# Windowed attention with sinks and a max-of-three FFN on one core: the opening in another order, its masks on TensorE, Q turned in one transfer

## The chip, the core and the metric

The kernel runs on one core of a Trainium2 chip. The core has a matmul engine (TensorE, PE), a vector engine (VectorE, DVE), a scalar engine that also evaluates exp (ScalarE, ACT), a general engine (GpSimd, POOL) and a sync engine that here only issues transfers (SyncE, SP). Each takes its instructions in order; what they hand over goes through semaphores. Sixteen DMA engines move data between HBM and on-chip memory. ScalarE, GpSimd and SyncE can issue transfers; those that change the type on the way (weights, float32 to bfloat16) are issued from GpSimd here. The metric is device time in microseconds, the median over runs. Lower is better.

## The reference

Attention over 4 batches, 8 heads, 768 positions, 64 dimensions. A position sees the first 4 positions (sinks) and the last 128. The result, as 3072 tokens of 512 features, goes through three projections to 768 features, their elementwise maximum, and a projection back:

```python
scores = scale * np.matmul(q, k.transpose(0, 1, 3, 2))
keep = is_sink | in_window            # pos < 4, or 0 <= rel < 128
a = softmax(np.where(keep, scores, -1e9))
x = (a @ v).transpose(0, 2, 1, 3).reshape(B * S, H * D)
h = np.maximum(np.maximum(x @ w1, x @ w2), x @ w3)
out = h @ w_out
```

## The kernel before

The work is cut into 12 chunks of 256 positions, three per batch (chunk `ci` is part `c = ci % 3` of batch `b`). A chunk has two blocks of 128 queries; heads go in four pairs `p`. All engines' orders are the order in which the program emits the calls; nothing is rescheduled, but each engine runs ahead of the others as far as its semaphores let it.

The steps of a chunk, each a function:
- `load` (L67) fetches k, q, v in float32, 512 KB each, into `k_raw`, `q_raw`, `v_raw` (two buffers each, so chunk `ci` waits for the casts of `ci - 2`).
- `cast_qk`, `cast_v` (L86, L95) make bfloat16 copies, in two and four instructions, from chunk 2 on GpSimd.
- `turn` (L100) transposes k and q on TensorE, with a copy out by VectorE (k) or ScalarE (q); `turn_dma` (L113) does it with DMA transposes issued by SyncE, two for k and two for q, 64 partitions each. `kT`, `qT` and `vb` are rings of four.
- `score` (L199) writes transposed scores (keys on partitions) of a pair into two banks `st`; `expo` (L218) takes the exponential on ScalarE and multiplies it by a 0/1 mask (`msk`, for a batch's first chunk `msk0`) on VectorE.
- `sink_k` (L176, GpSimd) copies the first four keys of a batch into `ks`; `sink_score` (L225) gives scores against them for the chunks that are not a batch's first, `sink_v` (L239) gathers the values of these keys.
- `av_open`, `av` (L251, L266) multiply with v, with the sum of the weights as a 65th column; VectorE takes the reciprocal and scales into `x_sb`.
- `xpose` (TensorE, copies by ScalarE) or `xpose_dma` (one DMA transpose) turn x into `xT`.
- `ffn_h(ci, fp, wi)` (L307) is one third of one projection: 8 matmuls of 256 columns; ScalarE copies the first projection to `h_sb`, VectorE takes the maximum with the others. `ffn_y` (L326) is half of the output projection, 6 matmuls of 512 columns, copied out by ScalarE; `store` (L335) issues the output.

PSUM has 8 banks, given out in turn; a bank's ninth user waits for the first to be read.

The opening (L350 to L433) is written out by hand for chunks 0 to 2. Masks are made by GpSimd first. Chunk 0's k halves are fetched from SyncE's queue and its q halves from ScalarE's. Casts of chunk 0 stand on VectorE. The four weights are issued by GpSimd, two behind chunk 0's v casts, one behind chunk 1's q casts, and the last (`wo`) behind chunk 1's v casts. Chunk 2's loads have a gate: VectorE writes one element of each buffer first, behind the mask products of chunk 1's second pair. Chunks 3 and 4 follow as buffers come free.

From L435 a loop does iteration `i` from 2 to 11: casts of chunk `i+2`, loads of `i+3`, DMA turns of `i+2`, then, with `n = i + 1`, `sink_k` and `sink_v` where `n` is the second chunk of a batch, sinks and scores of `n`, the output projection of `i - 1`, exponentials of `n`, projections of `i` mixed with `av` of `n`, and x of `n` turned by DMA. On GpSimd `sink_k` therefore stands behind the casts of chunk `i + 2`, and on TensorE `sink_score(n)` and all behind it wait for `ks`.

Of the kernel before, what the change touches and what calls it, by code (L numbers as in the profile page):

```python
# [16 lines left out]
def kernel(  # L17
# [31 lines left out]
    with tc.manual_schedule():  # L49
# [10 lines left out]
        qT = [const.tile([128, 2, NP, 2, 64], BF16, name=f"qT{i}") for i in range(RING)]  # L60
# [6 lines left out]
        def load(ci, what="kqv", eng=None, parts=1, gate=None):  # L67
# [4 lines left out]
            for w in what:  # L72
                src = {"k": k, "q": q, "v": v}[w]
                if (ci, w) not in raws:
                    raws[ci, w] = raw.tile([128, H, 2, D], F32, tag=w + "_raw", name=w + "_raw")
                dst = raws[ci, w]
                if gate is not None:
                    gate.memset(dst[0:1, 0, 0, 0:1], 0.0)
                n = H // parts
                for g in range(parts):  # L80
                    (eng or nc.sync).dma_start(
                        out=dst[:, n * g:n * g + n],
                        in_=src[b, n * g:n * g + n, t0:t0 + 256]
                            .rearrange("h (p i) d -> p h (i d)", i=2))
# [15 lines left out]
        def turn(ci, w, g):  # L100

            pt = bank([128, 2, 2, 128], BF16, "pt")
            x = bfs[ci, w]
            for p in range(2):
                for i in range(2):
                    nc.tensor.transpose(  # L106
                        pt[:, p, i], x[:, 2 * g + p, i].rearrange("q a d -> q (a d)"), ident)
            dst = (kT if w == "k" else qT)[ci % RING]
            (nc.vector.tensor_copy if w == "k" else nc.scalar.copy)(
                dst[:, :, 2 * g:2 * g + 2].rearrange("q n p i r -> q n (p i) r"),  # L110
                pt.rearrange("q p i (n r) -> q n (p i) r", r=64))

        def turn_dma(ci, w):  # L113
            dst = (kT if w == "k" else qT)[ci % RING]
            x = bfs[ci, w].rearrange("q p i a d -> q (p i a d)")
            for n in range(2):
                nc.sync.dma_start_transpose(  # L117
                    out=dst[:, n].rearrange("q p i r -> q (p i) r"), in_=x[64 * n:64 * n + 64])
# [8 lines left out]
        sel = const.tile([128, 32], BF16, name="sel")  # L127


        msk = const.tile([128, 2, 4, 128], BF16, name="msk")  # L130
        msk0 = const.tile([128, 2, 3, 128], BF16, name="msk0")

        def masks():
            nc.gpsimd.memset(msk[:, 0, 0:2], 1.0)
            for i in range(2):
                hp = slice(64 * i, 64 * i + 64)
                nc.gpsimd.affine_select(
                    out=msk[hp, 0, 1], in_=msk[hp, 0, 1], compare_op=ALU.is_ge, fill=0.0,
                    base=-i, pattern=[[1, 2], [2, 64]], channel_multiplier=-2)
                nc.gpsimd.affine_select(  # L140
                    out=msk[hp, 0, 0], in_=msk[hp, 0, 0], compare_op=ALU.is_gt, fill=0.0,
                    base=i, pattern=[[-1, 2], [-2, 64]], channel_multiplier=2)
            nc.gpsimd.tensor_copy(msk0[:, 0, 0], msk[:, 0, 1])
            nc.gpsimd.tensor_copy(msk0[:, 0, 1], msk[:, 0, 0])
            nc.gpsimd.tensor_copy(msk0[:, 0, 2], msk[:, 0, 1])
            for i in range(2):
                nc.gpsimd.memset(msk0[64 * i:64 * i + 2, 0, 0:2], 1.0)
            nc.gpsimd.tensor_copy(msk0[:, 1], msk0[:, 0])

        def masks_late():  # L150
            nc.gpsimd.tensor_copy(msk[:, 0, 2:4], msk[:, 0, 0:2])
            nc.gpsimd.tensor_copy(msk[:, 1], msk[:, 0])

        bm = const.tile([128, 2], F32, name="bm")

        def sink_init():

            nc.gpsimd.memset(sel, 0.0)
# [25 lines left out]
        w_sb = []  # L184

        def load_w(wi):
            w = (moe_w1, moe_w2, moe_w3)[wi]
            wt = const.tile([128, DS, d_ff], BF16, name=f"w{wi}")
            nc.gpsimd.dma_start(out=wt, in_=w.rearrange("(a p) f -> p a f", p=128))
            w_sb.append(wt)  # L190
# [8 lines left out]
        def score(ci, pairs):  # L199
            b, c = divmod(ci, CPB)  # L200
            kc, qc = kT[ci % RING], qT[ci % RING]
            for p in pairs:
                st = [bank([128, 4, 128], F32, "st") for a in range(2)]
                for s, x, n, q0, q1 in ((0, kT[(ci - 1) % RING], 1, 0, 1), (1, kc, 0, 0, 2),
                                        (3, kc, 1, 1, 2)):
                    if s == 0 and c == 0:
                        continue
                    for a in range(2):
                        hp = slice(64 * a, 64 * a + 64)
                        nc.tensor.matmul(  # L210
                            st[a][:, s:s + q1 - q0],
                            lhsT=x[hp, n, p].rearrange("q i r -> q (i r)"),
                            rhs=qc[hp, q0:q1, p].rearrange("q n i r -> q n (i r)"),
                            start=True, stop=True)
# [303 lines left out]
```

## Time and profile before

| | |
|---|---|
| median of 3 runs | 205.19 us (204.28 to 205.7) |
| the profiled execution, its own time | 206.73 us |
| its span, first to last instruction | 205.0 us |
| mean granted TensorE clock | 0.958 |
| busy: TensorE, VectorE, ScalarE, GpSimd | 174.1, 111.5, 88.9, 71.9 us |
| HBM read and written | 25.17 MB, 6.29 MB |

How to read it: the rows of digits cut the span into 40 slices of 5.1 us, a digit is the busy share in tenths. A row of the chain of waits is start, duration, engine and what it did. A row of a timeline is start, duration, engine, line, operation, output<-inputs, form, count and, in brackets, how long the engine had stood idle and what ended that. A row of windows is the stretch, its length, then busy time (and instructions) of TensorE's matmuls, its weight loads, VectorE, ScalarE and GpSimd, the granted clock, the DMA share and GB/s. "SPq" and "POOLq" are issues of transfers on the queues of SyncE and GpSimd. The clock row is 1.00 from the start although the first transposes ran slower than later ones (0.62 us for four at 5.19, 0.89 us for sixteen at 43.36), so the early slices of that row are not a reading.

### The profile page before, as it was taken

How to read it: one execution, taken by the hardware profiler on the slowest of the kernel's cores; microseconds unless marked ns; L12 is line 12 of the kernel's file. 1: busy time of each engine (PE TensorE's matmuls, PEld its weight loads, DVE VectorE, ACT ScalarE, POOL GpSimd, SP SyncE). 2: the span in 40 equal slices, each digit the busy share in tenths (PEclk: the TensorE clock that was granted, in tenths of full speed). 3: DMA queues.
4: the chain of work that ended last, by engine and by line, in shares of the span. 5: the costliest groups of instructions: out<-in, count | busy, mean ns of one | idle time of the engine just before them, and what ended most of it. 6: DMA issues, size and time to landing. Idle time of an engine off the chain costs nothing.

```text
span 205.0 us, 4504 instructions
## 1 busy us (share of the span) xinstructions
PE 174.1 (85%) x1788; PEld 129.8 (63%) x1800; DVE 111.5 (54%) x239; ACT 88.9 (43%) x177; POOL 71.9 (35%) x139
## 2 busy tenths in 40 slices
PE   0345978999739999999967999999999899999990
PEld 0223755896624976858735958858678488685860
DVE  1247263264831683864934845937739368286340
ACT  2412772225423537348163148264272661742321
POOL 7298702779204602611802706408227000000000
PEclk9999995799976999999997999999999999999999
DMA  5999999993569829979999989789899963142404
GB/s 153 290 200 204 184 161 290 294 276 105 132 109 299 167 52 252 176 176 295 96 137 294 181 218 243 165 207 244 146 268 167 173 110 99 35 102 51 106 0 102
DMA packets 72436, 35.68 MB, mean 174 GB/s; under 512 B 30176, under 2 KB 69344, under 8 KB 72416
## 3 DMA queue, kind: packets, MB, share of 16 engines
q1 hardware_dynamic: 68992, 31.73, 74.1%
q0 software_dynamic: 2368, 3.15, 9.9%
q10 hardware_dynamic: 1056, 0.52, 1.0%
q8 instruction: 14, 0.23, 0.5%
q14 instruction: 6, 0.05, 0.1%
HBM read 25.17 MB, written 6.29 MB: 153 GB/s over the span
## 4 chain that ended last, share of the span: by engine, by line
PE 48%; DMA 14%; ACT 11%; DVE 10%; issue 8%; SPq 4%; POOL 2%; DVEq 0%
PE h_ps L314 30%; PE y_ps L331 8%; ACT e_sb L222 7%; DMA xT<-x_sb 5%; DMA qT<-q_bf 4%; PE st L210 4%; DVE h_sb L322 3%; DMA q_raw<-in_q_dram 3%; DVE x_sb L285 3%; SPq L117 3%; PE pt L106 2%; PE o L277 2%; DMA k_raw<-in_k_dram 2%; ACT y_sb L333 2%; DVE e_sb L223 2%
## 5 line engine op out<-in xcount | busy, mean ns | idle before, releaser
L314 PE MATMUL h_ps<-xT,w 128*128 128x256 bf16 x864 | 107.1, 280 | 3.2 <-DMA xT<-x_sb 3.2
L314 PEld LDWEIGHTS <-w 128*128 128x128 bf16 x864 | 83.6, 100 | 17.4 <-DMA xT<-x_sb 5.0
L223 DVE TENSOR_TENSOR e_sb<-e_sb,msk 128x1024 bf16<-128x1024 bf16 (+1 forms) x48 | 34.2, 712 | 58.9 <-ACT e_sb L222 55.9
L322 DVE TENSOR_TENSOR h_sb<-h_sb,h_ps 128x512 bf16<-128x512 bf16 x72 | 49.2, 683 | 18.6 <-PE h_ps L314 16.4
L222 ACT ACTIVATE e_sb<-st 128x512 bf16<-128x512 f32 (+1 forms) x96 | 49.4, 585 | 6.3 <-PE st L210 6.3
L320 ACT CAST h_sb<-h_ps 128x512 bf16<-128x512 f32 x36 | 21.6, 601 | 47.8 <-PE h_ps L314 47.8
L91 POOL CAST k_bf<-k_raw 128x512 bf16<-128x512 f32 x20 | 13.4, 694 | 70.6 <-issue 42.0
L331 PE MATMUL y_ps<-wo,h_sb 128*128 128x512 bf16 x132 | 34.2, 392 | 1.1 <-DVE h_sb L322 0.2
L96 POOL CAST vb<-v_raw 64x512 bf16<-64x512 f32 x48 | 31.2, 650 | 10.6 <-DMA v_raw<-in_v_dram 8.6
L331 PEld LDWEIGHTS <-h_sb 128*128 128x128 bf16 x144 | 13.7, 100 | 17.9 <-issue 3.9
L333 ACT COPY y_sb<-y_ps 128x512 f32<-128x512 f32 x24 | 14.2, 592 | 21.8 <-PE y_ps L331 11.0
L285 DVE TENSOR_TENSOR x_sb<-o,rc 128x256 bf16<-128x256 f32 x48 | 20.4, 425 | 1.7
L277 PE MATMUL o<-vb,e_sb 128*128 128x65 bf16 x352 | 18.7, 197 | 1.7 <-DVE e_sb L223 1.7
L210 PE MATMUL st<-qT,kT 64*128 64x128 bf16 (+1 forms) x256 | 15.0, 256 | 4.7 <-DMA qT<-q_bf 2.3
L277 PEld LDWEIGHTS <-e_sb 128*128 128x128 bf16 x352 | 16.3, 100 | 4.1 <-DVE e_sb L223 2.2
L91 POOL CAST q_bf<-q_raw 128x512 bf16<-128x512 f32 x22 | 14.8, 699 | 3.6 <-DMA q_raw<-in_q_dram 3.4
L210 PEld LDWEIGHTS <-kT 64*128 64x128 bf16 x256 | 10.3, 101 | 8.4 <-issue 7.0
L106 PE MATMUL pt<-ident,k_bf 128*128 128x128 bf16 x24 | 3.3, 280 | 8.1 <-DVE k_bf L91 8.1
L296 PE MATMUL xt<-ident,x_sb 128*128 128x128 bf16 x24 | 4.3, 280 | 4.9 <-DVE x_sb L285 4.8
L282 DVE RECIPROCAL rc<-o 128x4 f32<-128x4 f32 x48 | 8.4, 175 | 0.1
L297 ACT COPY xT<-xt 128x512 bf16<-128x512 bf16 x6 | 3.2, 588 | 11.7 <-PE xt L296 11.7
L236 ACT ACTIVATE e_sink<-sk 128x256 bf16<-128x256 f32 x8 | 3.1, 384 | 11.6 <-PE sk L231 11.6
(46 smaller groups left out, 44.1 us busy)
## 6 DMA issues: line engine op xcount, KB each, us to landing
v_raw<-in_v_dram SPq DMA_DIRECT2D x12, 512.0 KB, 7.1
k_raw<-in_k_dram SPq DMA_DIRECT2D x11, 512.0 KB, 5.8
q_raw<-in_q_dram SPq DMA_DIRECT2D x11, 512.0 KB, 6.6
out_dram<-y_sb SPq DMA_DIRECT2D x22, 256.0 KB, 4.0
w<-in_moe_w_dram POOLq DMA_DIRECT2D x3, 768.0 KB, 7.2
wo<-in_moe_w_out_dram POOLq DMA_DIRECT2D x1, 768.0 KB, 9.1
q_raw<-in_q_dram ACTq DMA_DIRECT2D x2, 256.0 KB, 5.0
k_raw<-in_k_dram SPq DMA_DIRECT2D x2, 256.0 KB, 4.4
```

Of the source, the lines that this page charges most:

```text
L91: eng.tensor_copy(x[:, 2 * g:2 * g + 2].rearrange("q p i a d -> q p a i d"), y[:, 4 * g:4 * g + 4].rearrange("q (p a) i d -> q p a i d", a=2))
L96: eng.tensor_copy(vb[ci % RING][64 * i:64 * i + 64, n, :, 0:D], raws[ci, "v"][64 * n:64 * n + 64, :, i])
L210: nc.tensor.matmul(st[a][:, s:s + q1 - q0], lhsT=x[hp, n, p].rearrange("q i r -> q (i r)"), rhs=qc[hp, q0:q1, p].rearrange("q n i r -> q n ...
L222: nc.scalar.activation(e[:, a, lo:], st[a][:, lo:], AF.Exp, scale=scale)
L223: nc.vector.tensor_mul(e[:, :, lo:], e[:, :, lo:], msk0 if lo else msk)
L277: nc.tensor.matmul(o[:, t, a], lhsT=e[:, a, s], rhs=vb[cv % RING][:, n, 2 * p + a], start=first, stop=True, skip_group_check=True)
L285: nc.vector.tensor_mul(xs[ci][:, :, p], o[:, :, :, 0:D], rc.unsqueeze(3).to_broadcast([128, 2, 2, D]))
L314: nc.tensor.matmul(hp[:, f].rearrange("q (t r) -> q t r", t=2), lhsT=w_sb[wi][:, ds, c0:c0 + 128], rhs=xTs[ci][:, :, ds], start=(ds == 0), ...
L320: nc.scalar.copy(dst, hp)
L322: nc.vector.tensor_max(dst, dst, hp)
L331: nc.tensor.matmul(yp, lhsT=hs[ci][:, fb, t * 128:(t + 1) * 128], rhs=wo[:, fb], start=(fb == 0), stop=(fb == FB - 1))
L333: nc.scalar.copy(ys[ci][:, t], yp)
```

## The change

It has five parts.

1. *Masks of chunks 0 and 1.* GpSimd and VectorE build additive masks `addm`, `addm0` (0 or -2^30). `score(..., add=True)` first writes the mask into the banks with a matmul against the identity and adds the scores to it; `expo(..., mul=False)` then leaves out VectorE's product. The 0/1 masks for later chunks are made from the additive ones on GpSimd (`masks_late`), behind the third weight.
2. *Opening order.* All loads of chunks 0 and 1 go out from SyncE's queue. ScalarE casts q of chunks 0 to 3, VectorE k of 0 and 1, and v of 0 and 1 is shared by VectorE and GpSimd. TensorE gets 8, 3 and 6 matmuls on zeros (`warm`) at three places, ScalarE an exponential of one element at the start. The calls of chunks 0 to 3 are written in another order; chunk 3 is turned on TensorE and the loop starts at `i = 3`.
3. *Transfers of the opening.* The first two weights follow GpSimd's half of chunk 0's v casts. Chunk 2's loads are gated by a copy on GpSimd that reads the second weight. The third weight goes in two halves, `wo` behind the k casts of chunk 2, and chunk 3's loads are gated behind the v casts of chunk 2.
4. *Q in one DMA transpose* of 128 partitions in place of two of 64; `qT` is laid out as pair, parity, block, position, and the score and sink matmuls read it with strides.
5. `sink_v` masks by using one selection matrix per head of the pair: 8 matmuls of 65 columns in place of 4 of 130 and a product; `bm` goes.

```diff
-        qT = [const.tile([128, 2, NP, 2, 64], BF16, name=f"qT{i}") for i in range(RING)]
+        qT = [const.tile([128, NP, 2, 2, 64], BF16, name=f"qT{i}") for i in range(RING)]
...
         def turn_dma(ci, w):
+            if w == "q":
+                nc.sync.dma_start_transpose(
+                    out=qT[ci % RING].rearrange("q p i n r -> q (p i) (n r)"),
+                    in_=bfs[ci, w].rearrange("s p i a d -> s (p i a d)"))
+                return
             for n in range(2):
...
-        load(0, "k", nc.sync, 2)
-        load(0, "q", nc.scalar, 2)
-        load(0, "v", nc.sync)
-        load(1, "kqv", nc.sync)
+        load(0, "kq", parts=2)
+        load(0, "v")
+        load(1)
...
+        def warm(n):
+            if n:
+                pw = bank([128, 512], F32, "warm")
+                for _ in range(n):
+                    nc.tensor.matmul(pw, lhsT=wz[:, 0:128], rhs=wz, start=True, stop=True)
...
+        def masks_late():
+            for a in range(2):
+                nc.gpsimd.tensor_scalar(msk[:, a], addm, 2.0 ** -30, 1.0, op0=ALU.mult, op1=ALU.add)
+            for a in range(2):
+                nc.gpsimd.tensor_scalar(msk0[:, a], addm0, 2.0 ** -30, 1.0, op0=ALU.mult, op1=ALU.add)
...
+        def score(ci, pairs, add=False):
...
+            if add:
+                m = addm if c else addm0
+                for p in pairs:
+                    for a in range(2):
+                        nc.tensor.matmul(sts[p][a][:, lo:], lhsT=ident, rhs=m,
+                                         start=True, stop=False, skip_group_check=True)
...
-            nc.vector.tensor_mul(e[:, :, lo:], e[:, :, lo:], msk0 if lo else msk)
+            if mul:
+                nc.vector.tensor_mul(e[:, :, lo:], e[:, :, lo:], msk0 if lo else msk)
...
+        warm(8)
+        masks()
+        sink_init()
         for g in range(2):
+            cast_qk(0, "k", g, nc.vector)
+            cast_qk(0, "q", g, nc.scalar)
+            turn(0, "k", g)
+            turn(0, "q", g)
+            score(0, range(2 * g, 2 * g + 2), add=True)
+        for p in range(NP):
+            expo(0, p, mul=False)
...
         load_w(0)
+        sink_k(0)
         load_w(1)
+        warm(3)
...
+        load_w(2, 0, d_ff // 2)
+        load_w(2, d_ff // 2, d_ff)
+        sink_v(0)
+        for p in range(NP):
+            expo(1, p, mul=False)
+        warm(6)
...
+        masks_late()
+
+        def after_w1(dst):
+            nc.gpsimd.tensor_copy(dst, w_sb[1][0:1, 0, 0:1])
+
+        load(2, gate=after_w1)
...
+        load_wo()
...
+        load(3, gate=pool_gate)
+        load(4)
...
+        store(0)
+        cast(3, q=nc.scalar)
...
+        store(1)
...
+        cast(4)
+        turn_dma(4, "k")
+        turn_dma(4, "q")
...
+        load(5)
...
-        for i in range(2, NCH):
+        for i in range(3, NCH):
```

SyncE's queue around chunk 5's loads (`k_raw_851` and its neighbours before). Before: chunk 4's loads, the store of chunk 0, the turns of chunk 3, then chunk 5's loads and the turns of chunk 4.

```order
L81 DMA v_raw_704<-in_v_dram 128x8x128
L338 DMA out_0_dram<-y_sb_709 64x2x512 x2
L117 DMA_TRANSPOSE kT3_72<-k_bf_690 128x8x64 x2
L117 DMA_TRANSPOSE qT3_76<-q_bf_693 128x8x64 x2
L81 DMA k_raw_851<-in_k_dram 128x8x128
L81 DMA q_raw_853<-in_q_dram 128x8x128
L81 DMA v_raw_855<-in_v_dram 128x8x128
L117 DMA_TRANSPOSE kT0_69<-k_bf_841 128x8x64 x2
L117 DMA_TRANSPOSE qT0_73<-q_bf_844 128x8x64 x2
L338 DMA out_0_dram<-y_sb_892 64x2x512 x2
```

Now (chunk 5's loads are `k_raw_1032` and its neighbours, the two stores those of chunks 0 and 1):

```order
L79 DMA v_raw_635<-in_v_dram 128x8x128
L364 DMA out_0_dram<-y_sb_776 64x2x512 x2
L364 DMA out_0_dram<-y_sb_875 64x2x512 x2
L122 DMA_TRANSPOSE kT0_69<-k_bf_977 128x8x64 x2
L117 DMA_TRANSPOSE qT0_73<-q_bf_980 128x8x128
L79 DMA k_raw_1032<-in_k_dram 128x8x128
L79 DMA q_raw_1034<-in_q_dram 128x8x128
L79 DMA v_raw_1036<-in_v_dram 128x8x128
L327 DMA_TRANSPOSE xT_1109<-x_sb_1060 128x8x128
```

The store of chunk 1 and the turns of chunk 4 moved ahead of chunk 5's loads, the turns of chunk 3 left the queue, and q's turn is one transfer.

GpSimd between the sinks' keys of the first batch and chunk 2's casts. Before, the first two weights (`w0_198`, `w1_200`) have gone out ahead of this piece, right behind chunk 0's four v casts; `q_bf_226` is chunk 1's q, `vb1_78` its v, `w2_230` the third weight, `k_bf_486` chunk 2's k:

```order
L180 COPY ks0_81<-kT0_69 64x4x4 x2
L151 COPY msk_105<-msk_105 128x256
L152 COPY msk_105<-msk_105 128x512
L91 CAST q_bf_226<-q_raw_95 128x2x2x2x64 x2
L189 DMA w2_230<-in_moe_w3_dram 128x4x768
L96 CAST vb1_78<-v_raw_97 64x8x64 x4
L195 DMA wo_108<-in_moe_w_out_dram 128x6x512
L91 CAST k_bf_486<-k_raw_370 128x2x2x2x64 x2
```

Now (`w1_118` is the second weight, `w2_119` the third in halves, `k_raw_498` to `v_raw_504` are chunk 2's buffers, `k_bf_520` its k, `vb2_79` its v):

```order
L195 COPY ks0_81<-kT0_69 64x4x4 x2
L204 DMA w1_118<-in_moe_w2_dram 128x4x768
L94 CAST vb1_78<-v_raw_97 64x8x64 x2
L204 DMA w2_119<-in_moe_w3_dram 128x4x384 x2
L175 TENSOR_SCALAR msk_114<-addm_112 128x512 x2
L177 TENSOR_SCALAR msk0_115<-addm0_113 128x384 x2
L431 CAST k_raw_498<-w1_118 1x1
L431 CAST q_raw_501<-w1_118 1x1
L431 CAST v_raw_504<-w1_118 1x1
L90 CAST k_bf_520<-k_raw_498 128x2x2x2x64 x2
L210 DMA wo_120<-in_moe_w_out_dram 128x6x512
L94 CAST vb2_79<-v_raw_504 64x8x64 x4
```

The sinks' keys moved between the first and the second weight, chunk 1's q casts and half of its v casts left GpSimd, four mask instructions and the three copies that gate chunk 2's loads came in behind the third weight, and `wo` moved behind chunk 2's k casts.

More of the change, by code (lines that the diff above doesn't have):

```diff
@@ L65, with load @@
         raws, bfs = {}, {}
-        def load(ci, what="kqv", eng=None, parts=1, gate=None):
+        def load(ci, what="kqv", gate=None, parts=1):
             if ci >= NCH:
@@ L100, in turn @@
         def turn(ci, w, g):
-            pt = bank([128, 2, 2, 128], BF16, "pt")
+            pt = bank([128, 4, 128], BF16, "pt")
             x = bfs[ci, w]
[L104 to L111, printed above, removed]
@@ L133, in masks @@
         def masks():
[L134 removed]
+            nc.gpsimd.memset(addm[:, 0:2], 0.0)
             for i in range(2):
@@ L378 @@
             av(0, p)
-        xpose(0, 0)
-        xpose(0, 1)
+            if p == 1:
+                for g in range(2):
+                    cast_qk(1, "k", g, nc.vector)
+        for g in range(2):
+            cast_qk(1, "q", g, nc.scalar)
         for g in range(2):
@@ L410 @@
             turn(2, "q", g)
[L411 to L412 removed]
+        ffn_h(1, 0, 2)
         sink_score(2)
[L414 to L416 removed]
+        score(2, (0, 1))
+        score(2, (2, 3))
         for p in range(NP):
             expo(2, p)
[L419 to L424 removed]
+        ffn_h(1, 1, 2)
+        ffn_h(1, 2, 2)
+        ffn_y(0, 0)
         av_open(2)
         av(2, 0)
[L427 removed]
         av(2, 1)
+        ffn_y(0, 1)
         av(2, 2)
[L430 removed]
         av(2, 3)
+        store(0)
+        cast(3, q=nc.scalar)
         xpose(2, 0)
         xpose(2, 1)
[L435 removed]
+        ffn_y(1, 0)
+        ffn_y(1, 1)
+        store(1)
+        for wi in range(3):
+            ffn_h(2, 0, wi)
+        for g in range(2):
+            turn(3, "k", g)
+            turn(3, "q", g)
+        score(3, (0, 1))
+        score(3, (2, 3))
+        cast(4)
+        turn_dma(4, "k")
+        turn_dma(4, "q")
+        expo(3, 0)
+        expo(3, 1)
+        ffn_h(2, 1, 0)
+        expo(3, 2)
+        ffn_h(2, 1, 1)
+        expo(3, 3)
+        ffn_h(2, 1, 2)
+        load(5)
+        ffn_h(2, 2, 0)
+        av_open(3)
+        av(3, 0)
+        av(3, 1)
+        ffn_h(2, 2, 1)
+        av(3, 2)
+        ffn_h(2, 2, 2)
+        av(3, 3)
+        xpose_dma(3)
+        for i in range(3, NCH):
             n = i + 1
             last = n >= NCH
+            load(i + 3)
             cast(i + 2)
[L439 to L442 removed]
+            turn_dma(i + 2, "k")
+            turn_dma(i + 2, "q")
             if not last:
@@ L447 @@
                 sink_score(n)
-                score(n, range(NP))
+                score(n, (0, 1))
+                score(n, (2, 3))
                 expo(n, 0)
```

195 lines of the change are left out of this document (90 added, 105 removed).

## Prediction, made before the changed kernel was run

> **What bounds the kernel now.** I read the page first, then the chain of waits in order of time, then the timelines of each engine up to the steady loop, then windows around the places where TensorE stood. The page:
>
> ```profile
> span 205.0 us, 4504 instructions
> PE   0345978999739999999967999999999899999990
> PEclk9999995799976999999997999999999999999999
> DMA  5999999993569829979999989789899963142404
> ```
>
> TensorE is full in most slices; the open ones are the first six (to 31 us), slice 11 (about 56 to 61) and the tail. The granted clock dips after each early gap. The chain of waits has the durations that I use as prices, and the moment from which both kernels do the same:
>
> ```profile
> 0.82 3.84 DMA k_raw<-in_k_dram
> 5.19 0.62 PE pt L106 x4
> 43.36 0.89 PE pt L106 x16
> 44.25 2.62 PE h_ps L314 x24
> 46.88 0.22 PE sk L231 x4
> 47.10 1.01 PE st L210 x24
> 75.01 0.17 PE sv L244 x4
> ```
>
> At 75.0 (`sv`) the loop body with `i = 3` begins: sinks and scores of chunk 4. The changed kernel reaches the same point with the same chunks finished, so from there both have 205.0 - 75.0 = 130.0 us of the same body, apart from Q's turn. The question is when it gets there. I call that moment T3; 75.0 before.
>
> **The opening on ScalarE.** The timeline of ScalarE before:
>
> ```profile
> 7.29 0.59 ACT L109 COPY qT<-pt 128x512 bf16<-128x512 bf16 x1 [4.06 <-PE pt L106]
> 15.01 1.64 ACT L222 ACTIVATE e_sb<-st 128x384 bf16<-128x384 f32 x4 [0.56 <-PE st L210]
> 20.48 1.07 ACT L297 COPY xT<-xt 128x512 bf16<-128x512 bf16 x2 [3.84 <-PE xt L296]
> 23.69 0.39 ACT L236 ACTIVATE e_sink<-sk 128x256 bf16<-128x256 f32 x1 [0.49 <-PE sk L231]
> 24.22 2.06 ACT L222 ACTIVATE e_sb<-st 128x512 bf16<-128x512 f32 x4 [0.15 <-PE st L210]
> ```
>
> and the windows for the load rate and for the clock:
>
> ```profile
> 2.40:13.00 10.60, 2.65 (x20) 1.54 (x20) 3.95 (x8) 3.06 (x6) 6.33 (x14) 1.00 1.15 285
> 55.60:58.78 3.18, 1.03 (x8) 0.57 (x8) 2.64 (x8) 0.12 (x1) 0.00 (x0) 0.96 0.70 111
> 58.78:65.66 6.88, 5.05 (x28) 2.34 (x27) 0.56 (x1) 2.70 (x7) 1.27 (x3) 0.52 0.95 230
> ```
>
> Moving chunk 0's q load from ScalarE's queue to SyncE's costs order, not bytes: at 285 GB/s a half (256 KB) takes 0.92 us. The first two halves landed at 4.66 after an issue at 0.82, so 2.0 us are latency; q's first half is now third: 0.82 + 2.0 + 3 x 0.92 = 5.6, say 6.0. From there ScalarE is the chain, since it now casts q: cast 0.59 (no row for it on ScalarE; taken as its copy of the same size, bounds 0.4 to 0.9), four transposes 0.62, qT copy 0.59, and the same for the second half: 9.6. Then a score gap of 0.5 and eight exponentials at 0.41: 13.4. Chunk 1: two q casts 1.2, two qT and two xT copies 2.1, sinks 0.39, eight exponentials at 0.51 = 4.1, handoffs 0.6: 21.8. The mask products are gone from this chain; the mask matmuls (8 of 384 and 8 of 512 columns) run on a TensorE that waits for ScalarE, as do the 17 warm-up matmuls, so I cost both at nothing; without that cover they would be 6.8 us (0.11 us for 256 columns by the 2.62 for 24 above). With x of the last pair, transposes and xT copies (2.4, prices below) the dense projections start at 24.3.
>
> **Weights.** The weights' issues on GpSimd, and the transfers' time to landing:
>
> ```profile
> 8.78 3.31 POOL L96 CAST vb<-v_raw 64x512 bf16<-64x512 f32 x4 [3.93 <-DMA v_raw<-in_v_dram]
> 12.04 1.65 POOL L189 DMA_DIRECT2D w<-in_moe_w_dram  x2
> 70.49 0.44 POOL L180 COPY ks<-kT 64x16 bf16<-64x16 bf16 x2
> 158.64 0.44 POOL L180 COPY ks<-kT 64x16 bf16<-64x16 bf16 x2
> DMA to landing us min/median/max: 6.9/7.2/10.0
> ```
>
> Two v casts instead of four stand ahead of the first weight: 8.78 + 1.65 + 0.83 = 11.3, then `sink_k` 0.44, the second weight out by 12.5 and landed by 12.5 + 10.0 = 22.5 at worst. That opens chunk 2's loads. The projections need the first weight at about 19, the second at 26.9 and the third at 32, so it is hidden. The four mask products that GpSimd now makes behind the third weight's issue have no row; between 0.5 and 1.2 each (half and twice its 64x512 cast of about 0.6 to 0.8) they end before 22.5, since v of chunk 1 is there by 13 at the rate above.
>
> **To the loop.** TensorE's and VectorE's prices: the four projection groups ahead of chunk 2's transposes are 4 x 2.62 = 10.5 (34.8), then transposes 0.89, a third of a group 0.87, sinks and scores 1.23: chunk 2's scores end at 37.8; before it was 47.10 + 1.01 = 48.1.
>
> ```profile
> 53.66 0.69 DVE L223 TENSOR_TENSOR e_sb<-e_sb,msk 128x1024 bf16<-128x1024 bf16 x1 [0.29 <-ACT e_sb L222]
> 55.41 0.68 DVE L322 TENSOR_TENSOR h_sb<-h_sb,h_ps 128x512 bf16<-128x512 bf16 x1
> 57.70 0.18 DVE L282 RECIPROCAL rc<-o 128x4 f32<-128x4 f32 x1
> 57.91 0.42 DVE L285 TENSOR_TENSOR x_sb<-o,rc 128x256 bf16<-128x256 f32 x1
> ```
>
> ScalarE's eight exponentials of chunk 2 end 37.4 + 4.1 = 41.5; VectorE's last mask product 42.2, two maxima that stand behind it 43.5, four pairs of reciprocal and product at 0.55 45.7, transposes 46.3. TensorE idles there again, but for shorter than at 56. Two outputs of chunk 1 (12 matmuls of 512 columns at 0.22, 2.7 with the handoff) 49.0, the copy 49.6. On TensorE follow one group 2.62, transposes and copies 1.8, scores 0.8, two groups 5.2 and the products with v 0.7: it is at T3 at about 60.2.
>
> **What is late next.** `sink_k(1)` stands on GpSimd behind the casts of chunk 5, before and after, and TensorE's first score at T3 reads it. SyncE's queue:
>
> ```profile
> 59.03 0.58 SPq L81 DMA_DIRECT2D k_raw<-in_k_dram  x1
> 161.96 2.54 SPq L117 DMA_TRANSPOSE kT<-k_bf  x2
> 164.59 2.54 SPq L117 DMA_TRANSPOSE qT<-q_bf  x2
> 167.22 1.27 SPq L338 DMA_DIRECT2D out_dram<-y_sb  x2
> 172.53 1.25 SPq L301 DMA_TRANSPOSE xT<-x_sb  x1
> ```
>
> Chunk 5's loads went out at 59.03 and `ks` was ready at 70.49 + 0.44 = 70.9: 11.9 us, hidden before, since TensorE came at 75.0. Now they stand behind the store of chunk 1, which waits for that copy at 49.6: store 1.3, kT 2.54, qT 1.25 (one whole-width turn, priced by xT's row): out at 54.8, `ks` at 66.7. So T3 = 66.7, not 60.2; the change moves the wait here. The DMA side does not come ahead of it: gate at 22.8, chunk 2 cast by 22.8 + 11.9 = 34.7, chunk 4's q five parts of 1.84 later and 2.0 latency, 45.9, cast by about 49; its turn is issued at 53.5.
>
> TensorE's 6.5 us idle also cost clock. Timeline of TensorE before:
>
> ```profile
> 60.61 1.47 PE L210 MATMUL st<-qT,kT 64*128 64x256 bf16 x16 [1.61 <-DMA qT<-q_bf]
> 62.84 3.58 PE L331 MATMUL y_ps<-wo,h_sb 128*128 128x512 bf16 x10 [0.22 <-issue]
> 102.81 0.84 PE L210 MATMUL st<-qT,kT 64*128 64x256 bf16 x16 [0.71 <-DMA qT<-q_bf]
> 103.71 2.75 PE L331 MATMUL y_ps<-wo,h_sb 128*128 128x512 bf16 x11
> 108.77 4.40 PE L314 MATMUL h_ps<-xT,w 128*128 128x256 bf16 x24 [2.31 <-DMA xT<-x_sb]
> 159.32 0.29 PE L231 MATMUL sk<-qT,ks 128*32 128x256 bf16 x4 [0.19 <-DMA qT<-q_bf]
> 164.30 2.79 PE L314 MATMUL h_ps<-xT,w 128*128 128x256 bf16 x24 [0.91 <-DMA xT<-x_sb]
> ```
>
> After the gap at 56 scores and outputs took 5.8 (60.61 to 62.84 + 3.58), at full clock 3.65 (102.81 to 103.71 + 2.75): 2.2 lost. [...]
>
> **Q in one transfer.** Each of the seven later chunks frees 2.54 - 1.25 = 1.3 us of SyncE's queue, behind which qT and xT go out. Waits and slow clock behind them in the rows above: 0.71 + 2.31 + (4.40 - 2.79) + 0.91 = 5.5. Each shortened by 1.3 gives 0.7 + 1.3 + 0.9 = 2.9; but `ks`, ready at 158.64 + 0.44 = 159.08, came 0.2 before its user at 159.32, so that round has no more to give. I take 2.0, bounds 0 and 5.5. The strided rows that the scores now read from qT, and `sink_v`'s eight small matmuls instead of four, I cost at 0 to 0.3.
>
> **Sum.** T3 66.7 - 75.0 = -8.3; clock +2.2; Q's turn -2.0: -8.1. The profiled span of 205.0 becomes 196.9, the profiled execution's 206.73 becomes 198.6. That execution was 1.5 above the median of the runs, 205.19; from the median I forecast 205.19 - 8.1 = 197.1.
>
> **Rivals.**
> *The wait for `ks` isn't there* (chunk 5 arrives in time, or its casts are quicker): T3 is TensorE's 60.2, no clock lost, 205.19 - 14.8 - 2.0 = 188.4. For it: nothing but the margins of my chain; against: the 11.9 us row would have to be 5.4. With half the wait it gives about 192. Chance 0.12.
> *Only the opening's gain is real and half of it goes to transfers*: chunk 3's gate and wo's late issue push chunk 4 back by 8 us or more, q's cast holds ScalarE ahead of chunk 2's xT copies. T3 72 to 76 and no gain from Q: 203.1 to 207.2. The DMA share is near full until 48 us in the page's row, which speaks for it; 4 us of slack in the estimate above against. Chance 0.08.
> *Slower: the second weight lands so late that the gate starves the opening.* From its landing L the chain is gate and chunk 2 (12.2), chunks 3 and 4 up to q (11.2), cast and turn (4.6), chunk 5 to `ks` (11.9): T3 = L + 40. That binds above L = 27 and is slower by over 1% from L = 37; at L = 40 T3 is 80 and the time 210.4. Against it: weights landed in 10.0 at most, and it takes 24. [...] Chance 0.06.
>
> **How the numbers follow.** The forecast, with its own range of 192 to 202.5 (T3 from 63.5 to 70.5, clock and Q by their bounds, not all at once), has 0.74. The range 190.5 to 202.5 adds half of the first rival: 0.80. One per cent of the time (2.05 us) is about what a measurement of this kernel can tell from no change. Faster by more than that (under 203.1): forecast and first rival, 0.86; within: 0.08; slower: 0.06.
>
> **What would show it.** Right: the last exponential of chunk 1 near 22 instead of 29; chunk 2's scores done near 38; chunk 5's loads out near 55; a TensorE gap of 4 to 8 us before the first `sk` of chunk 4, ended by GpSimd's `ks` copy, with the granted clock at half behind it; one qT turn of about 1.25 us per chunk on SyncE. Wrong: `sk` of chunk 4 near 60 with no gap (first rival), chunk 2's k cast after 33 or chunk 3's after 45 (the other two), or steady rounds that grow longer without these causes.

## The result: 198.9 us, 2.9% faster, and the profile after

The changed kernel takes 198.88 us (median; 197.69 to 199.98) beside 204.74 for the kernel before in the same comparison: a ratio of 0.971, 95% interval 0.962 to 0.979. The forecast was 197.1 with a range of 190.5 to 202.5. Ratios, here and below, leave disturbed runs out, so they are not always the quotient of the two medians. The profiled execution took 199.98 us, with a span of 198.2 (205.0 before). It is 1.1 us above its kernel's median and that of before 2.0 above, so about 1 us of what lies between the two profiles belongs to the executions.

The page of the changed kernel, the rows that answer to those shown of before:

```profile
span 198.2 us, 4630 instructions
PE   7698969998999079999989999999898999999990
PEclk9999999999999859999999999999999999999999
DMA  5999998998479999349969999799798952122404
```

The open slices at the start are nearly filled. The hole at slice 11 has gone, but there is a new one in slices 13 and 14, 64 to 71 us, with the clock's dip behind it. The timeline of TensorE around it, and its two landmarks ahead:

```profile
28.56 10.64 PE L340 MATMUL h_ps<-xT,w 128*128 128x256 bf16 x96 [0.94 <-ACT xT L323]
41.12 1.06 PE L233 MATMUL st<-qT,kT 64*128 64x128 bf16 x24
...
63.69 0.25 PE L270 MATMUL sv<-vb,sel 128*32 128x65 bf16 x8
70.78 0.41 PE L255 MATMUL sk<-qT,ks 128*32 128x256 bf16 x4 [6.84 <-POOL ks L195]
71.12 1.89 PE L233 MATMUL st<-qT,kT 64*128 64x128 bf16 x24
72.94 3.54 PE L357 MATMUL y_ps<-wo,h_sb 128*128 128x512 bf16 x12
85.57 0.29 PE L255 MATMUL sk<-qT,ks 128*32 128x256 bf16 x4
85.79 1.30 PE L233 MATMUL st<-qT,kT 64*128 64x128 bf16 x24
87.03 2.76 PE L357 MATMUL y_ps<-wo,h_sb 128*128 128x512 bf16 x12
```

TensorE had everything but the sinks' keys at 63.9 and stood 6.84 us for `ks`. The two queues that made it late, SyncE's and then GpSimd:

```profile
48.22 6.59 SPq L364 DMA_DIRECT2D out_dram<-y_sb  x4
54.92 3.19 SPq L122 DMA_TRANSPOSE kT<-k_bf  x2
58.20 1.26 SPq L117 DMA_TRANSPOSE qT<-q_bf  x1
59.52 0.58 SPq L79 DMA_DIRECT2D k_raw<-in_k_dram  x1
```

```profile
23.13 0.18 POOL L431 CAST k_raw<-w 1x1 f32<-1x1 bf16 x1 [3.25 <-DMA w<-in_moe_w_dram]
64.16 1.17 POOL L90 CAST k_bf<-k_raw 128x512 bf16<-128x512 f32 x2 [11.65 <-DMA k_raw<-in_k_dram]
67.66 2.57 POOL L94 CAST vb<-v_raw 64x512 bf16<-64x512 f32 x4 [0.52 <-DMA v_raw<-in_v_dram]
70.29 0.43 POOL L195 COPY ks<-kT 64x16 bf16<-64x16 bf16 x2
```

Stores of chunks 0 and 1 (6.59 us in one piece, the second waiting for its copy), the turns of chunk 4, only then chunk 5's loads at 59.52; their casts hold GpSimd until 70.2, and `ks` is copied behind them: 70.72, or 11.2 us after the loads.

So the 6.8 us between the spans come from three places. T3 (first `sk` of chunk 4) went from 75.01 to 70.78: -4.2. From there to the second `sk` (85.57) is 14.79 us against 13.53 before: +1.3, the slow clock (0.50 granted from 70.78 to 74.50). The six rounds behind it are shorter by 4.2, as the windows over them show, first before, then after (length, TensorE, its weight loads, VectorE, ScalarE, GpSimd, clock, DMA share, GB/s):

```profile
88.54:173.56 85.02, 79.54 (x859) 60.21 (x865) 52.97 (x111) 40.38 (x82) 27.41 (x44) 0.98 0.97 190
```

```profile
85.57:166.41 80.84, 78.34 (x875) 59.64 (x874) 52.16 (x111) 40.17 (x82) 27.98 (x44) 1.00 1.01 196
```

TensorE does the same work; 3.0 us less of the time is idle, and it is busy 1.2 us less, at a mean granted clock of 1.00 for 0.98. The tail adds 0.3. The DMA engines count as busy nearly all the time in both, so that share tells nothing; the rate does, 190 and 196 GB/s for nearly the same bytes (16.2 and 15.8 MB).

### The profile page after: what moved, and what is told of

The parts are those of the page before. It is cut to its first block, busy times and chain, and to the rows that moved or that the text cites. A ratio compares the mean times of both kernels' runs of the same rounds, so it can differ in the third digit from the quotient of the medians.

```text
span 198.2 us, 4630 instructions
## 1 busy us (share of the span) xinstructions
PE 176.6 (89%) x1865; PEld 129.7 (65%) x1865; DVE 108.1 (55%) x239; ACT 94.4 (48%) x188; POOL 64.4 (32%) x119
## 4 chain that ended last, share of the span: by engine, by line
PE 58%; DMA 13%; DVE 11%; ACT 7%; issue 4%; SPq 3%; POOL 2%; POOLq 0%; DVEq 0%
PE h_ps L340 31%; PE y_ps L357 11%; PE st L233 6%; DMA q_raw<-in_q_dram 5%; DVE h_sb L348 5%; ACT e_sb L245 4%; DMA v_raw<-in_v_dram 4%; PE o L303 3%; DVE x_sb L311 3%; DMA qT<-q_bf 2%; PE st L223 2%; PE pt L104 1%; SPq L79 1%; SPq L327 1%; DMA k_raw<-in_k_dram 1%
## 5 line engine op out<-in xcount | busy, mean ns | idle before, releaser
L340 PE MATMUL h_ps<-xT,w 128*128 128x256 bf16 x864 | 102.7, 273 | 1.0 <-ACT xT L323 0.9
L340 PEld LDWEIGHTS <-w 128*128 128x128 bf16 x864 | 81.8, 98 | 13.0 <-issue 1.4
L247 DVE TENSOR_TENSOR e_sb<-e_sb,msk 128x1024 bf16<-128x1024 bf16 (+1 forms) x40 | 27.8, 695 | 46.5 <-ACT e_sb L245 46.4
L245 ACT ACTIVATE e_sb<-st 128x512 bf16<-128x512 f32 (+1 forms) x96 | 48.5, 589 | 3.4 <-PE st L233 3.2
L94 POOL CAST vb<-v_raw 64x512 bf16<-64x512 f32 x44 | 28.8, 654 | 20.0 <-DMA v_raw<-in_v_dram 16.6
L303 PE MATMUL o<-vb,e_sb 128*128 128x65 bf16 x352 | 17.6, 193 | 0.1
L90 POOL CAST q_bf<-q_raw 128x512 bf16<-128x512 f32 x16 | 11.0, 714 | 2.3 <-DMA q_raw<-in_q_dram 2.1
L106 ACT COPY qT<-pt 128x512 bf16<-128x512 bf16 x8 | 4.5, 588 | 11.9 <-PE pt L104 11.9
L255 PE MATMUL sk<-qT,ks 128*32 128x256 bf16 x32 | 2.5, 296 | 8.0 <-POOL ks L195 7.6
L143 PE MATMUL warm<-wz 128*128 128x512 bf16 x17 | 6.2, 521 | 1.2 <-DVE wz L132 1.2
```

Of the source, the lines that this page charges most:

```text
L90: f(x[:, 2 * g:2 * g + 2].rearrange("q p i a d -> q p a i d"), y[:, 4 * g:4 * g + 4].rearrange("q (p a) i d -> q p a i d", a=2))
L94: eng.tensor_copy(vb[ci % RING][64 * i:64 * i + 64, n, :, 0:D], raws[ci, "v"][64 * n:64 * n + 64, :, i])
L245: nc.scalar.activation(e[:, a, lo:], st[a][:, lo:], AF.Exp, scale=scale)
L247: nc.vector.tensor_mul(e[:, :, lo:], e[:, :, lo:], msk0 if lo else msk)
L303: nc.tensor.matmul(o[:, t, a], lhsT=e[:, a, s], rhs=vb[cv % RING][:, n, 2 * p + a], start=first, stop=True, skip_group_check=True)
L340: nc.tensor.matmul(hp[:, f].rearrange("q (t r) -> q t r", t=2), lhsT=w_sb[wi][:, ds, c0:c0 + 128], rhs=xTs[ci][:, :, ds], start=(ds == 0), ...
```

## The experiments

A time is the median, and the kernel before had 205.0, 204.9, 204.5 or 203.8 us in the comparison.

**1 and 2. Is the wait for `ks` only a matter of order?** The first puts `sink_k` ahead of the casts in the loop, the second issues chunk 5's loads ahead of the store of chunk 1 and the turns of chunk 4.

```diff
         for i in range(3, NCH):
+            if not last and n % CPB == 1:
+                sink_k(n // CPB)
             cast(i + 2)
...
                 if n % CPB == 1:
-                    sink_k(n // CPB)
                     sink_v(n // CPB)
```

> The changed kernel with the copy of the sinks' keys on GpSimd put ahead of the casts of chunk i+2 in each round, nothing else. Theory: the 6.84 us in which TensorE stood before the first sink score of chunk 4 (63.9 to 70.8) are only the place of that copy behind chunk 5's casts. Then the sink scores start near 64, the clock stays at full (another 1.6), and the next limit is the turn of chunk 5's q, which lands near 77.5, about when TensorE needs it: 190.5 to 193.5 us, 0.93 to 0.945 of the kernel before. Rival: the arrival of chunk 5 sets the pace by itself; the wait goes to the scores of chunk 5 and the time stays within 2 us of 198.9.

```diff
+        load(5)
         store(1)
...
-        load(5)
```

> The changed kernel with chunk 5's loads issued behind the store of chunk 0, ahead of the store of chunk 1 and of chunk 4's turns; the copy of the sinks' keys stays behind chunk 5's casts. Theory (the wait is SyncE's queue plus 11.2 us from load to copy): loads out near 50 instead of 59.5, copy near 61, no gap at 64, the same time as with the copy put first, 190.5 to 193.5 us. Rival (the copy itself or the transfers' bandwidth): the loads land no earlier because chunk 4's turns and the stores share the engines, the gap stays above 3 us and the time above 195.

Measured: 190.82 us (0.932, interval 0.926 to 0.938) and 191.89 (0.934, 0.926 to 0.942), both in the range of the theory. TensorE's timeline of the first:

```profile
61.40 0.28 PE L255 MATMUL sk<-qT,ks 128*32 128x256 bf16 x4
67.02 2.79 PE L340 MATMUL h_ps<-xT,w 128*128 128x256 bf16 x24 [0.55 <-DMA xT<-x_sb]
77.31 0.29 PE L255 MATMUL sk<-qT,ks 128*32 128x256 bf16 x4 [0.96 <-DMA qT<-q_bf]
```

T3 is 61.40 without a wait (62.31 in the second), and the mean clock is 1.000 against 0.981. Either end of the chain from SyncE's queue over the loads and casts to `ks` can be cut, and 7 to 8 us come free. That was the forecast's mechanism, and it is shown. The first rival in the prediction gave 188.4 for a kernel without this wait, with T3 at 60.2.

**3 and 4. What is q's single transfer worth?** The third run takes it out of the changed kernel, the fourth puts it alone into the kernel before (the matmuls and copies that use the new layout change with it, not shown here).

```diff
             if w == "q":
-                nc.sync.dma_start_transpose(
-                    out=qT[ci % RING].rearrange("q p i n r -> q (p i) (n r)"),
-                    in_=bfs[ci, w].rearrange("s p i a d -> s (p i a d)"))
+                for n in range(2):
+                    nc.sync.dma_start_transpose(
+                        out=qT[ci % RING][:, :, :, n].rearrange("q p i r -> q (p i) r"),
+                        in_=bfs[ci, w][64 * n:64 * n + 64].rearrange("q p i a d -> q (p i a d)"))
```

> The changed kernel with q turned by two DMA transposes of 64 partitions again, nothing else. My sum gave the one transfer 2.0 us (bounds 0 and 5.5); the trace from the first sink score of chunk 4 to the end is 127.4 after 130.0, with some 1.6 lost to the clock in it, so up to 4.2 might be due to it. Theory: 200.5 to 203.5 us, with waits for qT or xT back in the rounds. Rival: the loop's gain is chance of where transfers met, not the turn: 198 to 200 us.

```diff
-        qT = [const.tile([128, 2, NP, 2, 64], BF16, name=f"qT{i}") for i in range(RING)]
+        qT = [const.tile([128, NP, 2, 2, 64], BF16, name=f"qT{i}") for i in range(RING)]
...
+            if w == "q":
+                nc.sync.dma_start_transpose(
+                    out=dst.rearrange("q p i n r -> q (p i) (n r)"), in_=x)
+                return
```

> The kernel before with only q's turn in one transfer (and its layout). Theory: the waits at chunk 5 and 6 (0.71 and 2.31 and the slow clock behind, 1.6) shrink: 0.98 to 0.995 of the kernel before, 200.7 to 203.7 us. Rival: no part of it in the end time, 0.995 to 1.005.

Measured: 205.5 (1.002, 0.998 to 1.006) and 199.14 (0.974, 0.968 to 0.981). Both expectations put the effect too low. Without the single transfer nothing that can be measured is left of the change; with it alone, the old kernel has a gain that can't be told from the whole change's (0.974 beside 0.971). Windows over the same six rounds, new opening with two turns, then old opening with one:

```profile
86.35:172.21 85.86, 78.28 (x869) 59.55 (x874) 52.06 (x111) 40.39 (x82) 26.64 (x44) 1.00 1.02 185
```

```profile
86.55:167.61 81.06, 78.19 (x859) 59.52 (x864) 51.87 (x111) 40.27 (x82) 26.93 (x44) 1.00 0.97 197
```

The rounds go with q's transfer, not with the opening: 85.9 (run 3) and 85.0 us (before) with two turns, 81.1 (run 4) and 80.8 (the changed kernel) with one. Where the 5 us sit with the new opening and two turns, on TensorE and on SyncE's queue:

```profile
70.39 0.40 PE L256 MATMUL sk<-qT,ks 128*32 128x256 bf16 x4 [8.11 <-POOL ks L196]
127.77 0.29 PE L256 MATMUL sk<-qT,ks 128*32 128x256 bf16 x4 [1.05 <-DMA qT<-q_bf]
142.74 0.84 PE L234 MATMUL st<-qT,kT 64*128 64x256 bf16 x16 [1.03 <-DMA qT<-q_bf]
157.90 0.29 PE L256 MATMUL sk<-qT,ks 128*32 128x256 bf16 x4 [1.60 <-POOL ks L196]
```

```profile
112.55 2.61 SPq L328 DMA_TRANSPOSE xT<-x_sb  x1
115.21 0.58 SPq L79 DMA_DIRECT2D k_raw<-in_k_dram  x1
...
118.95 3.78 SPq L123 DMA_TRANSPOSE kT<-k_bf  x2
122.82 3.13 SPq L118 DMA_TRANSPOSE qT<-q_bf  x2
126.05 1.30 SPq L365 DMA_DIRECT2D out_dram<-y_sb  x2
127.46 2.71 SPq L328 DMA_TRANSPOSE xT<-x_sb  x1
```

SyncE's queue has no hole here: this round of issues takes 14.9 us, while TensorE's own work of a round is 13.0 (78.28 / 6). The issue of the two k turns behind the three loads takes 3.78, with no loads ahead of them 2.54 (the row at 161.96 in the prediction). That points to the queue as what sets the pace once the opening lets TensorE arrive early, so that the gain is returned in waits; runs 6 and 9 to 11 test it. Note the `ks` wait of 1.60 at the last batch (chunk 10): the wait of the opening comes back in the loop when casts run late.

**5. Old opening, one turn, keys first.** The kernel of run 4, with `sink_k` ahead of the casts.

```diff
+            if not last and n % CPB == 1:
+                sink_k(n // CPB)
             cast(i + 2)
```

> The kernel before with q's turn in one transfer and with the sinks' keys copied ahead of the casts; its opening stays. Theory: with the old opening TensorE comes to that copy last, so putting it first changes nothing against q's turn alone (199.14): 197.5 to 200, and the rewritten opening is worth what lies between this and 190.8. Rival: the copy's place costs every kernel, and this comes to 196 or less.

Measured: 200.26 (0.978, 0.968 to 0.988), the same as without the keys first (199.14 and 0.974; the intervals overlap): with the old opening TensorE comes too late to wait for `ks` (one wait of 0.35 us in run 4's profile, none in run 5's). Set against run 1, which differs in the opening and in `sink_v`'s small matmuls, the new opening is worth 9 us (4.8% by the two ratios) once both the `ks` order and q's turn are right. In the change as it was made, its worth can't be told from nothing.

**6. Is it the time on SyncE's queue as such?** In the kernel before, the stores of chunks 2 to 10 were issued by GpSimd.

```diff
-                nc.sync.dma_start(out=dst[i, :, t0:t1], in_=ys[ci][64 * i:64 * i + 64, t0:t1])
+                (nc.sync if ci < 2 or ci == NCH - 1 else nc.gpsimd).dma_start(
+                    out=dst[i, :, t0:t1], in_=ys[ci][64 * i:64 * i + 64, t0:t1])
```

> The kernel before with q turned in two transfers as it was, but the stores of chunks 2 to 10 issued from GpSimd's queue in place of SyncE's. It frees about 1.3 us of SyncE's queue per round, as q's single transfer does, and leaves the transposes alone. Theory (SyncE's time to issue paces the rounds): the round falls from 14.2 towards 13.5 us and the time to 199 to 202. Rival (the second transpose's own work on the transfer engines): round and time stay, 203.5 to 206.5.

Measured: 204.84 (1.007, 1.002 to 1.012). This is the rival's case. The six rounds took 84.8 us in its profile (85.0 before), so the theory that any time taken off that queue shortens the rounds fell. A reading that fits, and that runs 9 to 11 test: the stores stand behind q's turn in the queue, so they are not on the way from the turn of x, over three loads and two k turns, to qT. The issues on that way took longer instead (12.3 to 13.9 us from xT's issue to the end of qT's, 10.6 to 12.6 before).

**7 and 8. What do the warm-ups and the mask matmuls cost?** Run 1 without the later warm-ups (3 and 6 matmuls), and run 1 without the 16 mask matmuls, so that chunks 0 and 1 are not masked.

```diff
-        warm(3)
...
-        warm(6)
```

> The kernel with the sinks' keys copied first (190.82), without the 3 and the 6 warm-up matmuls; the first 8 stay. The prediction cost them at nothing; the chain of waits of the changed kernel has 1.08 and 1.40 us of them. Theory: they are on the path and the clock does not need them: the dense projections start 1.4 to 2.5 us earlier, 188.3 to 189.8. Rival (they keep the clock up): projections run at half clock for 2 us or more, 191 to 193.5.

```diff
-            score(0, range(2 * g, 2 * g + 2), add=True)
+            score(0, range(2 * g, 2 * g + 2))
...
-        score(1, (0, 1), add=True)
-        score(1, (2, 3), add=True)
+        score(1, (0, 1))
+        score(1, (2, 3))
```

> The kernel with the sinks' keys copied first (190.82), without the 16 mask matmuls of chunks 0 and 1, which then go unmasked (the output differs for that). The prediction cost them at nothing, behind ScalarE; the chain of waits has four groups of them, 1.28, 1.28, 0.97 and 0.97 us. Theory: the first two stand in front of exponentials, the others partly: TensorE reaches the sinks of chunk 4 2 to 4 us earlier, 187 to 189. Rival (ScalarE sets the pace, as forecast): within 0.7 of 190.8.

Measured: 190.47 (0.937, 0.929 to 0.945) and 190.59 (0.937, 0.930 to 0.944), beside 190.82 (0.932) for run 1. The first lies between its two expectations, the second in its rival's. Neither can be told from nothing, but the intervals leave room for about 2 us. The profiles say a little more. The dense projections begin at 25.96 us in both, although TensorE ran slowly there until about 10 and 12 us (eight score matmuls took 0.82 us at 8.49 in run 7 and at 10.20 in run 8, 0.51 at 7.96 in run 1); with warm-ups and masks they begin at 27.74 in run 10 and 28.56 in the changed kernel after a slow start like these, and at 25.95 in run 12 after a fast one. Of the difference q's earlier arrival is 0.3 and 0.4 us. So the two seem to be free only when TensorE is at full speed early; one profile each does not prove it.

**9 and 10. The order in the queue.** If the way to qT is too long because three loads stand in it, moving the turns of chunk `i+2` ahead of the loads of `i+3` should do what the single transfer does. Run 9 does it in the kernel before (two turns of q, with the keys first as well), run 10 in run 1.

```diff
             cast(i + 2)
-            load(i + 3)
             turn_dma(i + 2, "k")
             turn_dma(i + 2, "q")
+            load(i + 3)
```

> The kernel before, q still in two transfers, but in the loop the four turns of chunk i+2 stand ahead of the loads of chunk i+3 on SyncE's queue (and sink_k ahead of the casts, which alone was worth nothing with one q transfer on the old opening). Theory (the chain on SyncE's queue from the turn of x, over the loads, to the turns of k and q paces the rounds): with about 2.6 us of loads out of that chain the seven waits for qT go, a round falls from 14.2 to 13.3-13.6 us as with one q transfer, and the time is 198-200.5 us. Rival (it is the second transpose's own work in the DMA engines that costs, wherever it stands): a round stays at 14.0-14.3 and the time at 203-206 us.

> The kernel after with sink_k ahead of the casts (190.8 us) and, in addition, the turns of chunk i+2 ahead of the loads of chunk i+3 in the loop. Theory (same chain): the waits left for qT (0.96 and 0.24 us) go and the time is 188.5-190.5 us; round 13.2-13.4. Rival: the chain no longer paces anything with one q transfer, and the later loads make casts and ks late: 190.5-192.5 us.

Measured: 202.45 (0.996, 0.991 to 1.002), between the two expectations, and not to be told from before; 190.53 (0.939, 0.933 to 0.945), the same as run 1 and at the border of both expectations. TensorE's timeline of run 9 (an execution of 205.39 us, the longest of its twelve) shows why so little came of it:

```profile
94.52 2.79 PE L314 MATMUL h_ps<-xT,w 128*128 128x256 bf16 x24 [1.29 <-DMA xT<-x_sb]
108.83 2.79 PE L314 MATMUL h_ps<-xT,w 128*128 128x256 bf16 x24 [1.18 <-DMA xT<-x_sb]
122.61 2.79 PE L314 MATMUL h_ps<-xT,w 128*128 128x256 bf16 x24 [0.95 <-DMA xT<-x_sb]
```

The waits for qT in the rounds are gone, as the theory said, but xT, which now has four transposes directly behind it, lands late. The view of transfers has the median from issue to landing last in its row, before and in run 9:

```profile
xT<-x_sb SPq DMA_TRANSPOSE x9, 3.3
```

```profile
xT<-x_sb SPq DMA_TRANSPOSE x9, 5.2
```

Runs 10 and 11, with the same order, show it too: xT's median is 4.0 and 4.8 us there, and 3.2 in run 1. The turn of x with three or four transposes directly behind it landed later in these runs, and what was spared for q was paid in part for x (run 3, with three loads directly behind it, has 4.0 too); whether that happens in the queue or in the DMA engines no run here shows. In the six rounds of run 9 together, 2.2 us were won (82.86 against 85.02).

**11. New opening, two turns, but both orders mended** (run 3 with `sink_k` ahead of the casts and the turns ahead of the loads, the diffs of runs 1 and 10).

> The new opening with q turned in two transfers (205.5 us), but in the loop with sink_k ahead of the casts and the turns ahead of the loads. Theory (the new opening's gain was lost in the loop because the chain on SyncE's queue, with the second turn of q in it, ran longer than TensorE's round; with the loads out of that chain it no longer does): the wait of 8.1 us for ks is gone, rounds 13.5-13.8, 192-195.5 us. Rival (the second transposes' work in the DMA engines itself holds the loop back): rounds 14.0 or more, 197-203 us.

Measured: 194.43 (0.958, 0.950 to 0.965), the theory's case: 4.4% better than run 3 by the two ratios, 9 to 11 us. The rounds' window:

```profile
77.28:159.21 81.93, 78.12 (x875) 59.15 (x874) 51.86 (x110) 40.28 (x82) 30.20 (x50) 1.00 0.98 202
```

and run 10's, which differs only in q's single transfer:

```profile
78.38:157.87 79.49, 78.01 (x874) 59.32 (x874) 52.05 (x110) 40.20 (x82) 30.08 (x49) 1.00 0.99 206
```

Two turns cost 2.4 us more in the rounds and 3.9 in the median (2.0% by the two ratios) even where no loads stand in front of them. The opening's gain is not lost to q's second turn alone, then: of the 15 us between run 3 and run 10, the two orders bring back 11 with the second turn still there. The single transfer alone brought 6.6 (run 3 to the changed kernel), so the shares depend on what is mended first. The two edits were not run apart with two turns, so their shares stay open too.

**12. The clock in the opening.** Four more matmuls on zeros fill TensorE's gap before the first q transposes, in run 10.

```diff
             turn(0, "k", g)
+            warm(0 if g else 4)
             turn(0, "q", g)
```

> The kernel of the run before (keys first, turns first; 190.5 us) with four more matmuls on zeros between the first k transposes and the first q transposes, where TensorE otherwise stands 1.2 to 2.3 us waiting for q's cast. Theory (in the opening TensorE's clock falls back to half or stays there because of that gap, and rises at 7 in one execution and at 10 to 13 in another): full clock from about 7 us in every execution, dense projections start at 25.5-26.3, the time 189-190 us. Rival (the moment at which the clock rises doesn't hang on that gap): full clock at 10 to 13 again, 190-191 us.

Measured: 189.44 (0.936, 0.932 to 0.940), all runs between 189.24 and 190.23, where run 10 spread from 189.48 to 193.81. TensorE's timeline of the changed kernel at that place, then of this run:

```profile
4.59 0.63 PE L104 MATMUL pt<-ident,k_bf 128*128 128x128 bf16 x4
6.84 0.60 PE L104 MATMUL pt<-ident,q_bf 128*128 128x128 bf16 x4 [1.61 <-ACT q_bf L90]
7.23 1.49 PE L223 MATMUL st<-addm,ident 128*128 128x384 bf16 x4
10.23 1.49 PE L223 MATMUL st<-addm,ident 128*128 128x384 bf16 x4
11.65 0.82 PE L233 MATMUL st<-qT,kT 64*128 64x256 bf16 x8
```

```profile
5.01 1.22 PE L143 MATMUL warm<-wz 128*128 128x512 bf16 x4
7.05 0.40 PE L104 MATMUL pt<-ident,q_bf 128*128 128x128 bf16 x4 [0.82 <-ACT q_bf L90]
7.28 0.81 PE L223 MATMUL st<-addm,ident 128*128 128x384 bf16 x4
10.11 0.50 PE L233 MATMUL st<-qT,kT 64*128 64x256 bf16 x8
```

Four mask matmuls take 1.49 us in one profile and 0.81 in the other, eight score matmuls 0.82 and 0.50. So here TensorE is at its full speed from 7.3, and in the changed kernel's profile not yet in the last row, which ends at 12.5. Run 1, with the changed kernel's opening to the letter, had 0.81 at 7.13. Run 3, with the same opening, had 0.81 at 7.10 and 1.49 again at 9.26: the speed was reached and lost. So one profile of an opening is a draw. That the filled gap ended the draw fits the narrow spread of six runs, but the trace is of one of them, and the ratio's interval overlaps run 10's: it is likely, not shown. By the median it is the fastest of these kernels, 4.7% under the changed one (3.6% by the two ratios).

## Why the prediction was right, and where only the sum was

The median came out 1.8 us above the forecast, in the range, and the likeliest case is the one that happened. Its terms, against the two spans:

| term | forecast | measured |
|---|---|---|
| T3, the new opening up to `ks` | -8.3 | -4.2 |
| clock behind the wait | +2.2 | +1.3 |
| q in one transfer | -2.0 (0 to 5.5) | -4.2 in the six rounds |
| tail | 0 | +0.3 |
| sum | -8.1 | -6.8 |

- **The mechanism was right.** "The change moves the wait here": a TensorE gap of 6.5 us ended by `ks` was forecast, 6.84 was found, and runs 1 and 2 show that the order alone makes it. The time from chunk 5's loads to `ks` was put at 11.9 and took 11.2. ScalarE's cast of q (0.59; 0.62 by its row) stands too, and the second weight nearly (22.5 at worst; the gate opened at 23.13). Masks and warm-ups at nothing is not refuted by the medians of runs 7 and 8, but holds to about 2 us only. The two rivals with late transfers didn't come up: chunk 2's k cast began at 28.9 and chunk 3's at 40.6, where 33 and 45 would have spoken for them.
- **The step that failed first: T3 was put 4.1 us too early**, and lies just past the range given to it (63.5 to 70.5). It is the opening's chain on ScalarE up to the dense projections: 24.3 was forecast, 28.56 measured, and this error of 4.3 goes through unchanged (chunk 2's scores end at 42.18 for 37.8, the outputs' copy at 53.54 for 49.6, `ks` 70.72 for 66.7). The timeline of ScalarE, then TensorE's two rows ahead of the projections:

```profile
6.16 0.62 ACT L90 CAST q_bf<-q_raw 128x512 bf16<-128x512 f32 x1 [3.92 <-DMA q_raw<-in_q_dram]
10.96 3.18 ACT L245 ACTIVATE e_sb<-st 128x384 bf16<-128x384 f32 x8
19.23 4.03 ACT L245 ACTIVATE e_sb<-st 128x512 bf16<-128x512 f32 x8 [0.38 <-PE st L233]
52.95 0.59 ACT L359 COPY y_sb<-y_ps 128x512 f32<-128x512 f32 x1 [0.71 <-PE y_ps L357]
```

```profile
26.02 0.41 PE L303 MATMUL o<-vb,e_sb 128*128 128x65 bf16 x8
27.17 0.45 PE L322 MATMUL xt<-ident,x_sb 128*128 128x128 bf16 x5 [0.57 <-DVE x_sb L311]
```

  The exponentials of chunk 1 ended at 23.26 instead of 21.8. That part goes with TensorE's speed: in run 1, where it was full early, they ended at 20.95. In run 8, slow early but without the mask matmuls, they ended at 21.35, so it is in part the masks, costed at nothing, running slowly. The rest, from there to the projections, was put at 2.5 us ("x of the last pair, transposes and xT copies") and took 5.3 in both profiles (20.95 to 26.25 in run 1): the products with v come in groups between thirds of a projection of 1.03 us each, and the transposes wait for the last of them (26.02, 27.17). This tail was taken for the last pair's alone, which is the mis-sized term, 2.8 of the 4.3.
- **The Q term was taken too small**, by an argument that the runs contradict: "`ks`, ready at 159.08, came 0.2 before its user, so that round has no more to give". A later round's `ks` is not a fixed time. It hangs on casts, loads and the buffers that turned chunks set free, all of which come earlier when the queue is shorter, round after round: in run 4 TensorE begins the same scores at 154.19 without a wait, where it was 159.32. Runs 3 and 4 give q's turn 5.9 to 6.6 us of the median (5.2 to 6.4 by the ratios), about or above the upper bound of 5.5.
- **The clock**: scores and outputs behind the wait took 5.36 us (71.12 to 76.48), the same work a chunk later 4.00 (85.79 to 89.79), so 1.4 were lost and not 2.2. From the first `sk` on the granted clock was 0.50 for 3.8 us, to about 74.5, and 1.00 from 75, a shorter stretch than the 6.88 us at 0.52 of before. The forecast's range also takes the clock by bounds, which no run shows. What the profile before shows is a gap of 0.71 us that cost none (1.00 granted from 102.81 to 106.46) and one of 2.31 us that cost 1.6 (24 matmuls in 4.40 us for 2.79, 0.61 granted from 108.77 to 113.20).
- **The sum held by luck, because errors cancelled**: the opening gave 4 us less, q's transfer 2 us more, the clock cost 1 us less. Two of the rivals' times also miss their own terms: T3 of 72 to 76 without a gain from Q gives 202.2 to 206.2 (203.1 to 207.2 was written), and T3 of 80 gives 210.2 (210.4); the forecast does not rest on them.
- **What the sum couldn't say**: the parts do not add. Alone, the opening is worth nothing that can be measured (run 3), q's transfer as much as the whole change (run 4); with the key copy in its place the opening is worth 9 us more (runs 1 and 5). The forecast treated them as independent terms.

## What to carry to other kernels

When an opening is made shorter, find what the loop's first iteration waits for, and what stands ahead of it in each queue: here one small copy behind eleven us of loads and casts kept 8 of 14 us (205 to 190.8). Price a transfer queue by its whole round against the busy engine's round; when the two are close, a gain ahead of the loop can come back as waits in it (in run 3 the queue's round was 14.9 us and TensorE's work 13.0), and moving one transfer forward can make its neighbour late, as xT in runs 9 to 11 (landed in 4.0 to 5.2 us for 3.2 and 3.3). A single wider transfer was worth more here than the waits that the profile had shown for it.

## What the runs showed of the hardware that was not expected

- Two DMA transposes of 64 partitions against one of 128, the same bytes: 85.9 and 80.8 us for six rounds (run 3 and the changed kernel), 81.9 and 79.5 with no loads ahead of them in the queue (runs 11 and 10). The two transposes read disjoint halves of the partitions, and one was quicker; whether the two ran one after the other no run shows.
- The issue of a transpose on SyncE wasn't of fixed length: two of k took 2.54 us with no loads ahead of them in the kernel before, and behind three loads in run 3 3.78 in the rows shown and 5.81 in the round after, so this queue's time can't be counted in issues alone.
- TensorE came to full speed at different times in executions of the same opening: four mask matmuls took 0.81 us at 7.13 in run 1's profile and still 1.49 at 10.23 in the changed kernel's, while the granted clock's row reads full in both from the first slice. In both a gap ended by q's cast (1.67 and 1.61 us) lies ahead of the first q transposes.
